# Common operand offsets, halved scaled states, filled waits, and rows moved by products in a fused attention and feed-forward kernel

## The chip, the core and the metric

The kernel runs on one core of a Trainium2 chip. The core's engines run at the same time and meet at semaphores: TensorE (PE in the profile, its weight loads PEld) multiplies a stationary tile with a moving one into PSUM, VectorE (DVE), ScalarE (ACT) and GpSimd (POOL) work elementwise, and SyncE (SP) issues the transfers between HBM and the on-chip SBUF. Each engine takes its instructions in the order in which the program lists them. The metric is the device time of one execution, in microseconds (us).

## What is computed

A gated linear attention (4 sequences, 8 heads, 768 steps, head size 48) and two feed-forward layers behind it, all in float32:

```python
def _attn_ref(q, k, v, alpha):
    for t in range(S):
        state = alpha[:, :, t, :, None] * state + np.einsum('bhd,bhe->bhde', k[:, :, t], v[:, :, t])
        y[:, :, t] = np.einsum('bhd,bhde->bhe', q[:, :, t], state)

def _moe_ref(x, w_in, w_out):          # 384 -> 2048 -> 384
    h = x @ w_in
    return (h * np.cos(h)) @ w_out

def _moe2_ref(x, w1, w2, w3, w_out):   # 384 -> 768 -> 384
    h = np.maximum(np.maximum(x @ w1, x @ w2), x @ w3)
    return h @ w_out
```

The attention's output, 3072 tokens of 8 x 48 features, is the first layer's x; the first layer's result is the second's.

## The kernel before

The 3072 tokens are cut into six units of 512 tokens (8 chunks of 64: two of each of the four sequences). Heads go in pairs p = 0 to 3. `att(u, k, p, t0)` does one pair of one unit, k = 0 to 3 standing for p = 3, 0, 1, 2: two scans on VectorE give the products of alpha within a chunk (g) and their scaled inverse, GpSimd scales k and q with them (L367 or L379, L382), TensorE transposes k (L387, copied out as kt in L390), forms q times k (L399) and k times v (L404), the first masked into a (L411 and L412 in unit 0, L415 later). VectorE then steps the state s from chunk to chunk (L421, L423). Each state is scaled by its chunk's g into d: in unit 0 by ScalarE, one instruction a chunk and head (L430); in later units by GpSimd, one a head (L435). `values` sums a times v (L449) and q times d (L455) into y. ScalarE writes y's high part into the layer's input tile xt (L470); the low part is what is left, in unit 0 by a product with minus identity (L473) and a copy (L475), later by a subtraction (L477). The pair p = 3 does not go to xt but to yy0: a pair's tile has 2 x 48 rows of its own and 2 x 16 free ones, and p = 3's 96 rows fill these, in before by two transfers for each of the other pairs (L484). In unit 0 all y share the two PSUM tiles acc0 and acc1.

Every operand of the feed-forward layers is a pair of float32r tiles, high and low, so each product is three instructions. A weight block arrives as 64-bit words (L307), VectorE turns it into float32 in three steps (L310 to L312), ScalarE takes the high part (L315) and GpSimd the low part (L316). `moe1(i)`, i = 16 u + f, computes h of one of the 16 blocks f of a unit by nine instructions (L497 to L499) of 128x512, the elementwise chain (L504 to L507 and, for i below GLP1 = 20, L509 to L511 with the low part on GpSimd, else L513, L514, L519 on VectorE), and nine instructions into the three accumulators (L524 to L526). The accumulators are written out at the unit's end (L533 to L536). `moe2_h` and `moe2_o` do the second layer (L574 to L586, L597 to L603).

The order is a planner's: `Program.order` gives every operation an estimated duration and a due time, simulates the engines, and the instructions are then emitted by simulated start, each engine's own in that order. The terms `W1E` (how many blocks ahead of its use a weight is due) and `MOE_EARLY` (how many blocks ahead the elementwise chain is due) are such due times; `PSUM` has five rotating banks ps0 to ps4 whose use the planner also settles. The layer-one weights wih, wil, woh, wol are allocated from the far end of SBUF, the attention's tiles from the near end behind xt, q, gh, gl, yy and raw. 16 products of the identity (L639) run first of all on TensorE.

Of the kernel before, what the change touches and what calls it, by code (L numbers as in the profile page):

```python
# [49 lines left out]
NQ, NG, NRAW, NIN, NV, NGS = 3, 2, 3, 3, 2, 3  # L50
NBANK = 5
# [7 lines left out]
GLP1 = 20  # L59
# [5 lines left out]
DAC = 1  # L65


W1E = 10
MOE_EARLY = 4
# [6 lines left out]
WARM, COLD, IDLE = 16, 7.0, 2.5  # L76


class Program:
# [38 lines left out]
    def order(self, banks, limit):  # L118
# [25 lines left out]
        start = [0.0] * n  # L144
        dma_free = 0.0
# [17 lines left out]
        for _ in range(n):  # L163
            t, e = min((max(free[e], min(map(ready, w))), e) for e, w in waiting.items() if w)
            assert t < never
            i = min((self.ops[j][5], j) for j in waiting[e] if ready(j) <= t)[1]
            waiting[e].remove(i)
            _, dur, nbytes, _, _, _, port = self.ops[i]
            start[i] = t
            if e == "PE":  # L170
                if t - free[e] > IDLE:
                    cold = t + COLD
                dur += min(dur, max(0.0, cold - t) / 2)
            free[e] = t + dur
            end = t + dur
            if port:
                port_free = end
            if nbytes is not None:
                dma_free = max(dma_free, end + (0.65 if e == "SP" else 1.05)) + nbytes / 260e3
                end = dma_free + 0.9  # L180
            for k in opens.get(i, ()):
                f = min(range(limit[k[1]]), key=lambda f: freed_at[k[1]][f])
                m = single(t)
                chosen[k] = m
                bank_end[k] = (m, f, 0.0)
                freed_at[k[1]][f] = never
                bank_free[m] = never
            for k in bank_of[i]:
                m, f, last = bank_end[k]
                last = max(last, end + self.SEM)  # L190
                bank_end[k] = (m, f, last)
                open_left[k] -= 1
                if not open_left[k]:
                    freed_at[k[1]][f] = last
                    bank_free[m] = last
            for u in users[i]:
                lag = self.LAG.get((e, self.ops[u][0]), self.SEM)
                ready_at[u] = max(ready_at[u], end + lag)
# [42 lines left out]
def tile_kernel(ctx, tc, qka, vv, wt, outT):  # L241
# [20 lines left out]

    q_b = [mp.tile([P, HB], F32, name=f"q{i}") for i in range(NQ)]
    gh_b = [mp.tile([P, HB], F32R, name=f"gh{i}") for i in range(NG)]
    gl_b = [mp.tile([P, HB], F32R, name=f"gl{i}") for i in range(NG)]
    yy_b = [mp.tile([P, 2, HB], F32R, name=f"yy{i}") for i in range(2)]
# [4 lines left out]
    one0 = ap.tile([PR, NC, C1], F32, name="one0")  # L271
    inv0 = [ap.tile([PR, NC, C1], F32, name=f"inv{i}") for i in range(2)]
    tri = ap.tile([P, 1, C], F32, name="tri")
    al_b = [ap.tile([PR, KO], F32, name=f"al{i}") for i in range(NIN)]
    kq_b = [ap.tile([PR, 2 * HB], F32, name=f"kq{i}") for i in range(NIN)]
    g_b = [ap.tile([PR, AL], F32, name=f"g{i}") for i in range(NGS)]
# [60 lines left out]
    def att(u, k, p, t0):  # L337
# [87 lines left out]
        for c in range(NC - 1):  # L425
            op("DVE", 0.2, lambda c=c: state(c), [rk[c % 2], *kgs, (*sk, c)], [(*sk, c + 1)], t0 + 0.25)
            if u < DAC and not firsts[c + 1]:
                for j in range(2):
                    w = slice(UP * j, UP * j + D)
                    op("Act", act(D) + 0.09, lambda c=c, j=j, w=w: se.activation(d[w, j, c + 1], s[w, c + 1], AF.Copy, scale=g[w, c + 1, 0:1]),  # L430
                       [*kgs, (*sk, c + 1)], [(dk, j, c + 1)], t0 + 0.25)
        if u >= DAC:
            for j in range(2):
                w = slice(UP * j, UP * j + D)
                op("Pool", pool(NC * D), lambda j=j, w=w: ge.tensor_tensor(d[w, j], s[w], g[w, :, 0:1].to_broadcast([D, NC, D]), ALU.mult),  # L435
                   [*kgs, *[(*sk, c) for c in range(NC)]], [(dk, j, c) for c in range(NC)], t0 + 0.25)
        elif not firsts[0]:
            for j in range(2):
                w = slice(UP * j, UP * j + D)
                op("Act", act(D) + 0.09, lambda j=j, w=w: se.activation(d[w, j, 0], s[w, 0], AF.Copy, scale=g[w, 0, 0:1]), [*kgs, (*sk, 0)], [(dk, j, 0)], t0 + 0.25)  # L440
# [15 lines left out]

        op("PE", 3 * SWITCH + N2 * mm4(C) + NC * mm4(C), values, [vk, ("a", n2, 0), ("a", n2, 1), *[(dk, j, c) for j in range(2) for c in range(NC)], kq], [*yks, ("done", n2)], t0 + 0.3)
# [4 lines left out]
        else:  # L462
# [3 lines left out]
            xa = [("xtA", xn)]  # L466
        for h in range(2):
# [11 lines left out]
        if p < NP - 1:  # L479
# [67 lines left out]
    def open_np():  # L547
# [58 lines left out]
    def build():  # L606
# [19 lines left out]

        def setup_rest():
# [132 lines left out]
```

## Time and profile before

| | us |
|---|---|
| three runs, lowest, median, highest | 829.34, 831.05, 832.0 |
| the profiled execution | 831.06 |
| its span, from the first to the last instruction | 829.3 |
| TensorE busy | 805.4 |
| VectorE busy | 477.7 |
| ScalarE busy | 372.5 |
| GpSimd busy | 189.0 |
| granted TensorE clock, mean over the span | 0.979 |

A busy time counts an instruction from its start to its modelled end, and TensorE's instructions overlap, so its 805.4 us do not say how fast it goes; the distance between two starts does. The share of a span also mixes stages: the profile has a start of some 50 us with attention of unit 0 and the first weights, a stretch to some 130 us in which the remaining weights, the attention of units 1 and 2 and the first blocks run together, the rest of layer one to some 530 us, and layer two.

### The profile page before, as it was taken

The numbers are of one execution on the slowest core, as the hardware profiler recorded it, in microseconds if no ns is written. First come the engines' busy times: TensorE is split into PE (matmuls) and PEld (weight loads), VectorE is DVE, ScalarE is ACT, GpSimd is POOL, SyncE is SP. The second block draws the span as 40 slices with busy tenths as digits, with TensorE's granted clock in tenths as the row PEclk, the third lists the DMA queues.
The fourth block names the chain that finished last, engine by engine and source line by source line (L and its number), as shares of the span: only waits on it lengthen the run. The fifth ranks groups of instructions, "written<-read, shape, count | busy, mean of one in ns | idle before, by whom it ended". The sixth has DMA issues, their size and how long they took to land.

```text
span 829.3 us, 15144 instructions
## 1 busy us (share of the span) xinstructions
PE 805.4 (97%) x6168; PEld 649.1 (78%) x6168; DVE 477.7 (58%) x924; ACT 372.5 (45%) x695; POOL 189.0 (23%) x187
## 2 busy tenths in 40 slices
PE   7689999999999999999999999999999999999998
PEld 6567777878778877887788778888888888888886
DVE  7689999875786577657679954453122222322221
ACT  5865655645555554556466745521121211112121
POOL 6478777621231023102033200110000000000000
PEclk8589999999999999999999999999999999999999
DMA  9446764330242024102224610232020020200001
GB/s 281 137 133 193 208 188 150 117 106 12 73 146 65 1 76 143 43 1 74 65 86 134 238 45 2 104 106 77 26 88 19 22 89 25 77 26 13 13 26 38
DMA packets 26661, 71.86 MB, mean 87 GB/s; under 512 B 3488, under 2 KB 3488, under 8 KB 26592
## 3 DMA queue, kind: packets, MB, share of 16 engines
q1 hardware_dynamic: 26592, 70.90, 26.9%
q8 instruction: 48, 0.79, 0.4%
q14 instruction: 21, 0.17, 0.1%
HBM read 54.37 MB, written 14.16 MB: 83 GB/s over the span
## 4 chain that ended last, share of the span: by engine, by line
PE 84%; DVE 5%; POOL 4%; issue 3%; DMA 2%; ACT 1%; SPq 0%; DVEq 0%; POOLq 0%; ACTq 0%
PE ps L575 9%; PE ps L576 9%; PE ps L574 9%; PE acc L524 8%; PE acc L526 7%; PE ps L497 7%; PE acc L525 7%; PE ps L499 7%; PE ps L498 7%; PE ps L599 3%; PE ps L598 3%; PE ps L597 3%; PE ps L455 2%; PE ps L449 1%; PE ps L399 1%
## 5 line engine op out<-in xcount | busy, mean ns | idle before, releaser
L497 PE MATMUL ps<-xt,wih 128*128 128x512 f32 x288 | 117.7, 409 | 2.8 <-ACT q L506 1.7
L524 PE MATMUL acc<-gh,woh 128*128 128x512 f32 x288 | 117.5, 408 | 0.3 <-DVE yy L534 0.2
L499 PE MATMUL ps<-xt,wil 128*128 128x512 f32 x288 | 115.0, 399 | 1.4 <-POOL wil L316 1.4
L526 PE MATMUL acc<-gl,woh 128*128 128x512 f32 x288 | 114.4, 397 | 0.6 <-DVE gl L519 0.4
L498 PE MATMUL ps<-xt,wih 128*128 128x512 f32 x288 | 114.8, 399 | 0.0
L525 PE MATMUL acc<-gh,wol 128*128 128x512 f32 x288 | 114.0, 396 | 0.0
L504 ACT ACTIVATE q<-ps 128x512 int32<-128x512 f32 x96 | 57.2, 596 | 70.8 <-PE ps L499 70.2
L584 DVE TENSOR_TENSOR ps<-t,ps 128x512 f32<-128x512 f32 x36 | 25.0, 695 | 104.8 <-PE ps L576 104.7
L513 DVE SCALAR_TENSOR_TENSOR ps<-q,ps 128x512 f32<-128x512 f32 x76 | 52.7, 693 | 55.4 <-ACT q L507 55.2
L506 ACT ACTIVATE q<-q 128x512 f32<-128x512 f32 x96 | 60.6, 631 | 50.3 <-DVE q L505 49.6
L505 DVE SCALAR_TENSOR_TENSOR q<-q,ps 128x512 f32<-128x512 int32 x96 | 65.8, 685 | 28.0 <-ACT q L504 24.8
L585 ACT ACTIVATE h<-ps 128x512 fp32r<-128x512 f32 x36 | 21.5, 598 | 113.1 <-DVE ps L584 113.0
L519 DVE TENSOR_TENSOR gl<-ps,gh 128x512 fp32r<-128x512 f32 x76 | 52.1, 685 | 26.4 <-ACT gh L514 26.2
L497 PEld LDWEIGHTS ps<-xt,wih 128*128 128x128 f32 x288 | 54.6, 189 | 16.2 <-ACT q L506 2.2
L499 PEld LDWEIGHTS ps<-xt,wil 128*128 128x128 f32 x288 | 54.6, 190 | 15.3 <-POOL wil L316 2.1
L524 PEld LDWEIGHTS acc<-gh,woh 128*128 128x128 f32 x288 | 54.2, 188 | 15.0 <-DVE yy L534 1.1
L582 DVE TENSOR_TENSOR t<-t,ps 128x512 f32<-128x512 f32 x36 | 24.7, 687 | 71.4 <-PE ps L576 70.7
L526 PEld LDWEIGHTS acc<-gl,woh 128*128 128x128 f32 x288 | 54.2, 188 | 14.6 <-DVE gl L519 0.8
L514 ACT ACTIVATE gh<-ps 128x512 fp32r<-128x512 f32 x76 | 45.3, 597 | 42.8 <-DVE ps L513 39.9
L498 PEld LDWEIGHTS ps<-xt,wih 128*128 128x128 f32 x288 | 54.8, 190 | 11.8
L525 PEld LDWEIGHTS acc<-gh,wol 128*128 128x128 f32 x288 | 54.3, 189 | 11.7
L435 POOL TENSOR_TENSOR d<-s,g 48x384 f32<-48x384 f32 x40 | 34.6, 864 | 122.7 <-DVE s L423 121.1
(122 smaller groups left out, 1595.2 us busy)
## 6 DMA issues: line engine op xcount, KB each, us to landing
raw<-in_wt SPq DMA_DIRECT2D x56, 384.0 KB, 3.4
kq<-in_qka SPq DMA_DIRECT2D x23, 448.0 KB, 4.5
x1d<-yy SPq DMA_DIRECT2D x18, 512.0 KB, 2.8
xt<-x1d SPq DMA_DIRECT2D x18, 512.0 KB, 4.3
v<-in_vv SPq DMA_DIRECT2D x22, 256.0 KB, 3.5
al<-in_qka SPq DMA_DIRECT2D x24, 228.4 KB, 3.0
outT<-y SPq DMA_DIRECT2D x18, 256.0 KB, 2.0
xt<-yy SPq DMA_DIRECT2D x36, 64.0 KB, 2.7
```

The costliest lines, as they stand in the source:

```text
L497: pe.matmul(ps, wi["h"][:, f, cc], xt[:, cc, 0], start=(cc == 0), stop=False)
L498: pe.matmul(ps, wi["h"][:, f, cc], xt[:, cc, 1], start=False, stop=False)
L499: pe.matmul(ps, wi["l"][:, f, cc], xt[:, cc, 0], start=False, stop=(cc == NR - 1))
L504: op("Act", act(HB, True), lambda: se.activation(q.bitcast(I32), ps, AF.Copy, scale=INV2PI), [hk], [qk], m)
L505: op("DVE", dve(HB), lambda: ve.scalar_tensor_tensor(q, q.bitcast(I32), -TWOPI, ps, ALU.mult, ALU.add), [hk], [qk], m)
L506: op("Act", act(HB), lambda: se.activation(q, q, AF.Sin, scale=0.5), (), [qk], m)
L524: pe.matmul(acc[c], oh, gh, start=(f == 0), stop=False)
L525: pe.matmul(acc[c], ol, gh, start=False, stop=False)
L526: pe.matmul(acc[c], oh, gl, start=False, stop=(f == NF1 - 1))
L574: pe.matmul(ps, w2t["h"][m][:, f, cc], xt[:, cc, 0], start=(cc == 0), stop=False)
L575: pe.matmul(ps, w2t["h"][m][:, f, cc], xt[:, cc, 1], start=False, stop=False)
L576: pe.matmul(ps, w2t["l"][m][:, f, cc], xt[:, cc, 0], start=False, stop=(cc == NR - 1))
```

## The change

Seven things change together.

*Offsets.* A pad of 88 floats is allocated behind the layer-one weights and one behind the layer-two tiles on the far side, and the attention's tiles that are read by scans get rows of 544 floats. In the built programs the byte offsets within a partition are these:

| tiles | before | after |
|---|---|---|
| xt, gh, gl, w of layer two (near side), modulo 512 | 128 | 128 |
| wih, wil, woh, wol, modulo 512 | 480 | 128 |
| h2, wo2 of layer two, modulo 512 | 480 | 128 |
| kq of attention, modulo 128 | 32 | 0 |
| a, v, kt, s, d, modulo 128 | 0 | 0 |

*Scaled states.* In unit 0 ScalarE now makes d for the first head of a pair only (DAH = 1); the second head's is one GpSimd instruction, as in later units.

*Rows by products.* In unit 0 the 16-row pieces of pair 3 are no longer transferred: a selection matrix for each pair (built by ScalarE in the tile gl1) is multiplied with yy0 and summed into y before the pair's y is read.

*Fills.* Where the planner saw TensorE idle ahead of an operation that opens a bank, or of `values`, and before 48 us of its own time, up to ten products of the identity are put into the bank first.

*Numbers.* GLP1 goes from 20 to 28, W1E from 10 to 8, MOE_EARLY from 4 to 5, and one estimated duration changes.

```diff
+PAD = 88
+LINE = 544
-GLP1 = 20
+GLP1 = 28
+DAH = 1
+SELU = 1
-W1E = 10
-MOE_EARLY = 4
+W1E = 8
+MOE_EARLY = 5
+FILL, NFILL, SPARE = 48.0, 10, 0.3
...
             if e == "PE":
+                gap[i] = t - free[e]
...
     wo = {n: wp.tile([P, NF1, DM], F32R, name=f"wo{n}") for n in "hl"}
+    wp.tile([P, PAD], F32, name="pad")
...
+    sel = gl_b[1][:, 0:(NP - 1) * P].rearrange("p (k n) -> p k n", k=NP - 1)
...
-    al_b = [ap.tile([PR, KO], F32, name=f"al{i}") for i in range(NIN)]
+    al_b = [ap.tile([PR, LINE], F32, name=f"al{i}")[:, 0:KO] for i in range(NIN)]
...
             if u < DAC and not firsts[c + 1]:
-                for j in range(2):
+                for j in range(DAH):
...
-        if u >= DAC:
-            for j in range(2):
+        for j in range(2):
+            if u >= DAC or j >= DAH:
                 w = slice(UP * j, UP * j + D)
                 op("Pool", pool(NC * D), lambda j=j, w=w: ge.tensor_tensor(d[w, j], s[w], g[w, :, 0:1].to_broadcast([D, NC, D]), ALU.mult),
...
+        moved = u < SELU and p < NP - 1
...
+        if moved:
+            def rest():
+                for h in range(2):
+                    for x in range(2):
+                        pe.matmul(y[h][:, 0:HB // 2], sel[:, p], yy_b[0][:, x, HB // 2 * h:HB // 2 * (h + 1)], start=False, stop=(x == 1), skip_group_check=True)
+
+            op("PE", 0.5, rest, ["sel", ("gl", 1), *[("yy0", x, h) for x in "hl" for h in range(2)]], yks, t0 + 0.3)
...
-        if p < NP - 1:
+        if p < NP - 1 and not moved:
...
+        np_.tile([P, PAD], F32, name="pad2")
...
+        def setup_sel():
+            for p in range(NP - 1):
+                se.activation(sel[:, p], ident, AF.Copy, scale=0.0)
+                for i in range(2):
+                    row = 16 * (2 * p + i)
+                    src = UP * (row // D) + row % D
+                    se.activation(sel[:, p, UP * i + D:UP * (i + 1)], ident[:, src:src + 16], AF.Copy)
+
+        op("Act", 2.4, setup_sel, ["ident"], ["sel", ("gl", 1)], due=-97)
...
+            if G.ops[i][0] == "PE" and plan.start[i] < FILL:
+                bank = ps_b[chosen[plan.opens[i][0]]] if i in plan.opens else acc[0] if G.ops[i][3].__name__ == "values" else None
+                for _ in range(min(NFILL, int((plan.gap[i] - SPARE) / 0.22)) if bank is not None else 0):
+                    pe.matmul(bank[:, 0:P], ident, ident, start=True, stop=True)
             G.ops[i][3]()
```

Three places show what this does to the order. On ScalarE, in unit 0 behind the first pair's a, the names are d for scaled states, kt for the transposed k, a for the masked products; before:

```order
L430 ACTIVATE d0_125<-s3_124,g0_112 48x48 x4
L390 ACTIVATE kt1_118<-ps3_100 128x448
L430 ACTIVATE d0_125<-s3_124,g0_112 48x48 x6
L411 ACTIVATE a1_120<-ps0_97 128x256
L430 ACTIVATE d0_125<-s3_124,g0_112 48x48 x4
L411 ACTIVATE a1_120<-ps4_101 128x256
L390 ACTIVATE kt0_117<-ps3_100 128x448
L430 ACTIVATE d1_126<-s0_121,g1_113 48x48 x7
```

After (L405, L426 and L445 are L390, L411 and L430 of before):

```order
L445 ACTIVATE d0_126<-s3_125,g0_113 48x48 x2
L405 ACTIVATE kt1_119<-ps3_101 128x448
L445 ACTIVATE d0_126<-s3_125,g0_113 48x48 x3
L426 ACTIVATE a1_121<-ps0_98 128x256
L426 ACTIVATE a1_121<-ps4_102 128x256
L445 ACTIVATE d0_126<-s3_125,g0_113 48x48 x2
L445 ACTIVATE d1_127<-s0_122,g1_114 48x48 x7
L405 ACTIVATE kt0_118<-ps3_101 128x448
```

The second pair's two a's stood behind ten and behind fourteen of the first pair's d's, and now both stand behind five.

On TensorE, at the end of the last pair of unit 0 (L455 or L469 is the last of its value products, L473 or L496 the product with minus identity, L497 to L499 or L520 to L522 layer one); before:

```order
L455 MATMUL acc1_95<-yy1_90,d1_126 48x64 x2
L387 MATMUL ps3_100<-ident_76,kq1_110 128x112 x4
L497 MATMUL ps2_99<-xt0_463,wih_78 128x512
L498 MATMUL ps2_99<-xt0_463,wih_78 128x512
L499 MATMUL ps2_99<-xt0_463,wil_79 128x512
L473 MATMUL acc0_94<-xt0_463,minus_77 128x256
L473 MATMUL acc1_95<-xt0_463,minus_77 128x256
```

After:

```order
L469 MATMUL acc1_96<-yy1_91,d1_127 48x64 x2
L487 MATMUL acc0_95<-yy0_90,gl1_89 128x256 x2
L487 MATMUL acc1_96<-yy0_90,gl1_89 128x256 x2
L520 MATMUL ps3_101<-xt0_480,wih_78 128x512
L521 MATMUL ps3_101<-xt0_480,wih_78 128x512
L522 MATMUL ps3_101<-xt0_480,wil_79 128x512
L496 MATMUL acc0_95<-xt0_480,minus_77 128x256
L496 MATMUL acc1_96<-xt0_480,minus_77 128x256
```

The four products with the selection (L487) stand between the value products and the reading of y; the transposes of the next unit's pair stand further on.

On TensorE, where the first three blocks' h are done and banks have to come free; before:

```order
L497 MATMUL ps1_98<-xt0_463,wih_78 128x512
L498 MATMUL ps1_98<-xt0_463,wih_78 128x512
L499 MATMUL ps1_98<-xt0_463,wil_79 128x512
L387 MATMUL ps2_99<-ident_76,kq0_109 128x112 x4
L497 MATMUL ps3_100<-xt0_463,wih_78 128x512
```

After:

```order
L520 MATMUL ps3_101<-xt0_480,wih_78 128x512
L521 MATMUL ps3_101<-xt0_480,wih_78 128x512
L522 MATMUL ps3_101<-xt0_480,wil_79 128x512
L734 MATMUL ps2_100<-ident_76 128x128 x10
L402 MATMUL ps2_100<-ident_76,kq2_112 128x112 x4
L734 MATMUL ps4_102<-ident_76 128x128 x3
L520 MATMUL ps4_102<-xt0_480,wih_78 128x512
```

Ten fills (L734) into bank ps2 now precede the transposes that open it, and three precede the product that opens ps4; there are 35 fills in all.

## Rows read from the trace of the kernel before

**Rows 1.** The page: engine table, busy tenths in 40 slices, granted clock.
```profile
PE 805.4 (97%) x6168; PEld 649.1 (78%) x6168; DVE 477.7 (58%) x924; ACT 372.5 (45%) x695; POOL 189.0 (23%) x187
...
DVE  7689999875786577657679954453122222322221
...
PEclk8589999999999999999999999999999999999999
```

**Rows 2.** Stretches: us, busy us of each engine, PEclk, DMA share, GB/s.
```profile
30.00:40.00 10.00, 7.59 (x127) 5.86 (x120) 5.07 (x14) 6.69 (x19) 6.12 (x6) 0.50 0.52 137
100.00:150.00 50.00, 47.75 (x495) 37.68 (x494) 47.51 (x103) 30.16 (x56) 34.74 (x31) 1.00 0.55 165
150.00:200.00 50.00, 50.00 (x503) 39.93 (x502) 35.33 (x70) 26.40 (x48) 18.51 (x16) 1.00 0.31 92
269.00:282.00 13.00, 13.00 (x60) 10.47 (x58) 6.56 (x10) 7.58 (x13) 0.00 (x0) 1.00 0.01 1
540.00:552.00 12.00, 12.00 (x54) 9.94 (x54) 9.43 (x17) 4.31 (x8) 3.10 (x3) 1.00 0.44 155
600.00:650.00 50.00, 50.00 (x221) 41.16 (x220) 12.44 (x18) 8.96 (x15) 0.00 (x0) 1.00 0.13 48
```

**Rows 3.** Timeline of TensorE, layer one: start, us, engine, line, operands.
```profile
269.65 0.40 PE L497 MATMUL ps<-xt,wih 128*128 128x512 f32 x1
...
281.36 0.40 PE L499 MATMUL ps<-xt,wil 128*128 128x512 f32 x1
```

**Rows 4.** Timeline of TensorE, layer two.
```profile
540.05 0.39 PE L576 MATMUL ps<-xt,w1l 128*128 128x512 f32 x1
...
551.84 0.39 PE L574 MATMUL ps<-xt,w1h 128*128 128x512 f32 x1
...
599.69 0.39 PE L597 MATMUL ps<-h,wo2h 128*128 128x512 f32 x1
...
601.50 0.40 PE L599 MATMUL ps<-h,wo2h 128*128 128x512 f32 x1
...
603.82 0.39 PE L574 MATMUL ps<-xt,w0h 128*128 128x512 f32 x1
...
615.83 0.39 PE L576 MATMUL ps<-xt,w2l 128*128 128x512 f32 x1
```

**Rows 5.** Timeline of TensorE, waits: in brackets the idle time before, and its releaser.
```profile
57.71 0.57 PE L387 MATMUL ps<-ident,kq 112*128 112x112 f32 x4 [2.00 <-DVE q L509]
...
94.03 0.47 PE L497 MATMUL ps<-xt,wih 128*128 128x512 f32 x1 [1.74 <-ACT q L506]
...
112.09 0.69 PE L449 MATMUL ps<-a,v 64*64 64x64 f32 x32 [1.21 <-DVE s L423]
124.18 0.47 PE L497 MATMUL ps<-xt,wih 128*128 128x512 f32 x1 [0.78 <-DVE q L509]
```

**Rows 6.** Groups of instructions: count, busy us, mean ns of one, idle before.
```profile
L519 DVE TENSOR_TENSOR gl<-ps,gh 128x512 fp32r<-128x512 f32 x76 | 52.1, 685 | 26.4 <-ACT gh L514 26.2
...
L435 POOL TENSOR_TENSOR d<-s,g 48x384 f32<-48x384 f32 x40 | 34.6, 864 | 122.7 <-DVE s L423 121.1
...
L430 ACT ACTIVATE d<-s,g 48x48 f32<-48x48 f32 x56 | 18.6, 332 | 1.3
...
L639 PE MATMUL acc<-ident 128*128 128x128 f32 x32 | 6.1, 378 | 1.4 <-POOL ident masks.py:199 1.4
```

**Rows 7.** Timeline of ScalarE in unit 0's attention.
```profile
7.95 0.54 ACT L390 ACTIVATE kt<-ps 128x448 f32<-128x448 f32 x1 [5.55 <-PE ps L387]
...
37.53 4.97 ACT L430 ACTIVATE d<-s,g 48x48 f32<-48x48 f32 x14
```

**Rows 8.** Timeline of VectorE, unit 0's states and layer one's first step.
```profile
24.33 0.26 DVE L423 SCALAR_TENSOR_TENSOR s<-s,g,ps 112x48 f32<-112x48 f32 x1 [2.76 <-ACT a L411]
...
36.97 0.21 DVE L421 COPY s<-ps 112x48 f32<-112x48 f32 x1 [4.47 <-ACT a L411]
...
53.57 0.69 DVE L505 SCALAR_TENSOR_TENSOR q<-q,ps 128x512 f32<-128x512 int32 x1 [0.41 <-ACT q L504]
```

**Rows 9.** The chain that ended last, around the last rows of unit 0: start, us, what.
```profile
48.38 0.51 SPq L484
...
48.95 2.88 DMA xt<-yy
...
51.96 0.47 PE ps L497
```

**Rows 10.** Who waited for whom on TensorE: us in total, times, longest.
```profile
PE ps L499 <- POOL wil L316: 1.4, 1, 1.4
```

More of the change, by code (lines that the diff above doesn't have):

```diff
@@ L144, in order @@
         start = [0.0] * n
+        gap = [0.0] * n
         dma_free = 0.0
@@ L202, in order @@
         self.start = start
+        self.gap = gap
+        self.opens = opens
         return sorted(range(n), key=lambda i: (start[i], i)), chosen
@@ L269, in tile_kernel @@
     ps_b = [pp.tile([P, 512], F32, name=f"ps{i}") for i in range(NBANK)]
-    one0 = ap.tile([PR, NC, C1], F32, name="one0")
-    inv0 = [ap.tile([PR, NC, C1], F32, name=f"inv{i}") for i in range(2)]
+    one0 = ap.tile([PR, LINE], F32, name="one0")[:, 0:AL].rearrange("p (c t) -> p c t", c=NC)
+    inv0 = [ap.tile([PR, LINE], F32, name=f"inv{i}")[:, 0:AL].rearrange("p (c t) -> p c t", c=NC) for i in range(2)]
     tri = ap.tile([P, 1, C], F32, name="tri")
-    al_b = [ap.tile([PR, KO], F32, name=f"al{i}") for i in range(NIN)]
+    al_b = [ap.tile([PR, LINE], F32, name=f"al{i}")[:, 0:KO] for i in range(NIN)]
     kq_b = [ap.tile([PR, 2 * HB], F32, name=f"kq{i}") for i in range(NIN)]
-    g_b = [ap.tile([PR, AL], F32, name=f"g{i}") for i in range(NGS)]
+    g_b = [ap.tile([PR, LINE], F32, name=f"g{i}")[:, 0:AL] for i in range(NGS)]
     v_b = [ap.tile([P, N2, 2, UP], F32, name=f"v{i}") for i in range(NV)]
@@ L427, in att @@
             if u < DAC and not firsts[c + 1]:
-                for j in range(2):
+                for j in range(DAH):
                     w = slice(UP * j, UP * j + D)
-                    op("Act", act(D) + 0.09, lambda c=c, j=j, w=w: se.activation(d[w, j, c + 1], s[w, c + 1], AF.Copy, scale=g[w, c + 1, 0:1]),
+                    op("Act", act(D) + 0.21, lambda c=c, j=j, w=w: se.activation(d[w, j, c + 1], s[w, c + 1], AF.Copy, scale=g[w, c + 1, 0:1]),
                        [*kgs, (*sk, c + 1)], [(dk, j, c + 1)], t0 + 0.25)
-        if u >= DAC:
-            for j in range(2):
+        for j in range(2):
+            if u >= DAC or j >= DAH:
                 w = slice(UP * j, UP * j + D)
@@ L436, in att @@
                    [*kgs, *[(*sk, c) for c in range(NC)]], [(dk, j, c) for c in range(NC)], t0 + 0.25)
-        elif not firsts[0]:
-            for j in range(2):
+            elif not firsts[0]:
                 w = slice(UP * j, UP * j + D)
-                op("Act", act(D) + 0.09, lambda j=j, w=w: se.activation(d[w, j, 0], s[w, 0], AF.Copy, scale=g[w, 0, 0:1]), [*kgs, (*sk, 0)], [(dk, j, 0)], t0 + 0.25)
+                op("Act", act(D) + 0.21, lambda j=j, w=w: se.activation(d[w, j, 0], s[w, 0], AF.Copy, scale=g[w, 0, 0:1]), [*kgs, (*sk, 0)], [(dk, j, 0)], t0 + 0.25)
         op("DVE", 0.2, lambda: state(NC - 1), [rk[1], *kgs, (*sk, NC - 1)], [(*sk, 0)], t0 + 0.27)
@@ L691, in tile_kernel @@
     chosen.update(chosen_)
+    plan = G
     build()
```

## The prediction

> **What bounds the kernel now.** I read the engine table and the forty slices first: TensorE is busy for 97% of the span, VectorE for 58%, but VectorE's digits stand at 8 and 9 from the third slice to the eighth, and the clock digit falls to 5 in the second [rows 1]. Then the busy time by stretch, which makes three stages of it [rows 2]. In 30 to 40 us the clock is at 0.50, the 1.2 GHz level, and TensorE has gaps. From 100 to 150 us VectorE works 47.51 of 50 us and TensorE 47.75: both are nearly full. From 150 us on TensorE is busy without a break and VectorE is not. The waits of TensorE that VectorE or ScalarE ends stand at 57.71, 94.03, 112.09 and 124.18 us [rows 5]; the last of these is the first product of block i = 14 (counted by groups of nine L497 to L499). So up to i = 14 the order on VectorE decides, and from there the number and the spacing of TensorE's instructions.
>
> The spacing is the main thing to see. In the first feed-forward layer 50 products of 128x512 start between 269.65 and 281.36 us [rows 3]: 0.2342 us each. In the second layer 53 start between 603.82 and 615.83 us [rows 4]: 0.2266 us each, the same shape, type and clock (1.00 in both). Eight products of L597 to L599, from 599.69 to 601.50 us, take 0.2263 us each. But ten products right behind the change from these to L574, 601.50 to 603.82 us, take 0.2320 us each, and then the rate is 0.2266 again.
>
> What differs is where operands lie. Modulo 512 bytes (one weight tile's row) the first layer's weights lie at 480 and the moving tiles at 128. In L574 to L576 both lie at 128, in L597 to L599 both at 480. So neither 128 nor 480 is slow by itself; the unequal pair is, and so are ten products behind a change of the pair. The neighbours' load is not the cause: from 540.05 to 551.84 us 52 products start 0.2267 us apart [rows 4] with VectorE busy 9.43 of 12 us and the DMA share at 0.44, while the slow stretch has 6.56 of 13 us and 0.01 [rows 2].
>
> **The change part by part.** The profiled execution is 831.06 us, of which 829.3 are its span; the median of the three runs is 831.05, so the two need no correction.
>
> *Offsets of the first layer.* The pad puts its weights at 128 too. If they then go at 0.2266, each product saves 7.6 ns. From i = 14 on TensorE sets the pace: 82 blocks x 18 products x 7.6 ns = 11.2 us. The 14 blocks before would save 14 x 18 x 7.6 ns = 1.9 us, but there VectorE is full, so I count 0 (bounds 0 and 1.9).
>
> *Relocking.* Attention interrupts the products three times a pair (L387; L399 with L404; L449 with L455), 48 times in the 16 pairs of units 2 to 5. If each time ten products go at 0.2320 again, that gives back 10 x 5.4 ns = 0.05 us, 2.6 us in all; if none, 0. No row of before shows equal operands behind attention, so I take the middle, 1.3.
>
> *Offsets of the second layer.* The second pad puts h and wo2 at 128 as well, so the roughly 30 changes between L574 to L576 and L597 to L599 should vanish: 30 x 0.05 = 1.6 us saved; 0.8 if half remain, since no row says what else a change brings.
>
> *Split scaled states.* In unit 0 ScalarE makes the scaled states d in 56 steps of 332 ns, 18.6 us [rows 6]; 14 of them, 4.97 us, stand in one row behind the last pair's a [rows 7]. Half go (28 x 0.332 = 9.3 us), and GpSimd makes them in four steps of 864 ns [rows 6]. GpSimd's step waits for all states of its pair. The nine small ScalarE copies that build the selections stand ahead of the first kt, before which ScalarE idles 5.55 us [rows 7]; they cost nothing unless they pass that, and then the first kt is late. The order shows the effect: pair 1's two a's stood behind ten and fourteen of pair 0's d's, and now both stand behind five. VectorE waited 2.76 us at 24.33 and 4.47 us at 36.97 for exactly such a's [rows 8].
>
> *Rows by products in PSUM.* Six issues on SP go. The last pair's chain was issue at 48.38, landing at 51.83, product at 51.96 [rows 9]: 3.6 us. Four products of half a row for each of three pairs take their place; by the rate above, 128x256 is 0.11 us at full and 0.23 us at half clock, so 0.5 to 0.9 us a pair, ahead of ScalarE's reading. But VectorE runs almost without a break from there to its first step of layer one at 53.57 [rows 8], with 0.41 us idle ahead of it, so the landing was not what came last: this gain is worth only what VectorE's order lets through. By the order VectorE also has six states, two a's and a scan less ahead of that first step; it does them later, so the step itself comes earlier than the gain.
>
> *Fills.* 35 products of 128x128 are added. The 16 of the warm-up take 6.1 us [rows 6], 0.38 each, so 13.4 us in all. In a wait for an operand they are free and may hold the clock up. Not so where the wait is for a bank: 10 stand ahead of the transposes that open ps2 and 3 ahead of the product that opens ps4. The 2.00 us wait at 57.71 was ended by VectorE's last read of such a bank [rows 5], and a fill that writes the bank has to wait for that too. These 13 come on top: at most 13 x 0.38 = 5.0 us of TensorE, in a stretch where VectorE is the slower.
>
> *Start in sum.* VectorE's shift is the yardstick. At best both of its waits go, 7.2 us. At worst nothing of them goes through and 2 of the 5 us of fills show. I take 3 us earlier, nearer to the 4.47 us wait than to none, since the chain behind it (a, state, d, value products) keeps its other steps.
>
> *The rest.* Moving the products' low part of i = 20 to 27 to GpSimd takes 8 x 0.685 us [rows 6] from VectorE after 150 us, where it has room: 0. Early terms 8 and 5 for 10 and 4 only reorder; ahead of the first vector step of i = 13 as many conversions (L310 to L312) stand as before, one more or less. I count 0, with 1 us each way.
>
> Sum: -11.2 + 1.3 - 1.6 - 3 = -14.5, so **816.5 us**. Ends of this case: best 11.2 + 1.9 + 1.6 + 7.2 = 21.9, so 809.2; worst 11.2 - 2.6 + 0.8 - 2 = 7.4, so 823.7.
>
> **The rivals.** *The offsets do nothing.* For it: the two layers also differ in accumulators and in load, and ten products behind a change are slow with equal operands. Against it: L597's steady 0.2263 with both at 480. Then only the start is left: 831.1 - 3 = 828, between 824 and 833.
> The Trainium skill (TensorE: Matmul & The Clock Gate, Step-by-step: what each phase is for) says that TensorE has two read ports, so that "Loading the next tile's weights doesn't steal SBUF read bandwidth from the running matmul"; by that rule this rival holds, 828. The two spacings of equal products speak against it, though no row names the port.
>
> *The start is bound by TensorE, not by VectorE.* Then its lead goes through: block 0's last products could start 10.4 us earlier than 51.96, as the wait for the last pair's a, seven of its d's and the landing (4.5 + 2.3 + 3.6) all go. With 13.1 us for all 96 blocks and 1.6 that gives 831.1 - 25.1 = 806. Against it: VectorE at 95% up to 150 us.
>
> *Weights late, which ends slower.* Early term 8 asks for each weight two blocks later than 10. If the products then wait for GpSimd's low part as once in the trace, 1.4 us [rows 10], in every one of the first 16 blocks for both weights, that is 45 us; for one of them, 22 us: 831.1 - 14.5 + 22 = 838.6. It decides from 0.91 us a block on. Against it: the level count of conversions above, and a single such wait in the whole trace.
>
> **How the numbers follow.** Forecast 0.79; offsets do nothing 0.09; start bound by TensorE 0.08; weights late 0.04. The range is the forecast's own ends, 809 to 823.5: they hold nearly all of its chance and, of the rivals, only the near part of the early start's and of that at 828's, about 8 in 10 together. 0.3%, about what a measurement of this kernel can tell, is 2.5 us: faster means below 828.5. The forecast and the early start are faster (0.87), and half of the rival at 828 (0.05): 0.92. The other half stays within, 0.04; slower 0.04.
>
> **What would show it.** Right: L520 to L522 and L547 to L549 start 0.227 us apart, with a few of 0.23 behind attention, where 234 stood; no slow ten behind a change of layer-two lines; the first vector step of block 0 between 46 and 51 us; VectorE still full up to about 120 us, TensorE with more gaps there than before. Wrong: 0.234 kept (offsets), 13 fills on the chain with a gap before them, waits for wil or wol in the first 16 blocks, or a clock that stays at 1.00 from the start and carries TensorE's lead through.

## The result, and the profile after

| | before | after |
|---|---|---|
| median of the runs | 831.0 us (829.34 to 832.0) | 817.89 us (815.8 to 821.61) |
| profiled execution, its span | 831.06, 829.3 us | 817.95, 816.2 us |
| ratio | 1 | 0.9849 (95% 0.981 to 0.9888) |

The changed kernel is faster by 13.1 us by the medians (the ratio, of the means, makes it 12.5), where 14.5 were forecast (816.5). Run once more beside other kernels (below, e8) it was at 818.89 us, ratio 0.9848 (0.9828 to 0.9868).

Line numbers move with the edit. The first layer's products are now L520 to L522 and L547 to L549, the second's L598 to L600 and L621 to L623; the first vector steps are L528 and L532, the a's L426, the d's L445 (ScalarE) and L450 (GpSimd), the weight conversion L325 to L327, the fills L734.

From the page of after, the engine table, VectorE's digits and the granted clock, to be set beside [rows 1]:

```profile
PE 795.4 (97%) x6250; PEld 649.4 (80%) x6250; DVE 472.6 (58%) x916; ACT 362.6 (44%) x676; POOL 206.6 (25%) x199
...
DVE  7988999864786587667679955452232222322221
...
PEclk9999999999999999999999999999999999999999
```

The clock's 8 and 5 of [rows 1] are gone from the digits. Busy time by stretch of after (columns as in [rows 2]):

```profile
10.00:20.00 10.00, 8.93 (x218) 8.27 (x218) 8.41 (x28) 6.47 (x22) 8.95 (x10) 0.83 1.04 304
30.00:40.00 10.00, 8.36 (x98) 6.79 (x99) 9.19 (x23) 5.77 (x19) 8.15 (x8) 1.00 0.62 156
40.00:50.00 10.00, 6.26 (x97) 5.06 (x97) 8.32 (x14) 7.47 (x14) 5.78 (x5) 1.00 0.48 152
100.00:150.00 50.00, 47.01 (x435) 37.33 (x434) 47.40 (x101) 29.12 (x54) 38.24 (x32) 1.00 0.52 156
262.00:274.50 12.50, 12.50 (x56) 10.32 (x55) 6.16 (x9) 7.62 (x13) 0.00 (x0) 1.00 0.00 0
```

In 30 to 40 us VectorE works 9.19 of 10 us where it worked 5.07, and the clock is 1.00 where it was 0.50. In 100 to 150 us both engines stand where they stood.

TensorE's timeline of after, for [rows 3] to [rows 5]:

```profile
25.01 0.48 PE L520 MATMUL ps<-xt,wih 128*128 128x512 f32 x1
...
47.52 2.50 PE L734 MATMUL ps<-ident 128*128 128x128 f32 x20 [3.74 <-DVE q L532]
49.85 0.55 PE L402 MATMUL ps<-ident,kq 112*128 112x112 f32 x4
...
119.81 0.39 PE L520 MATMUL ps<-xt,wih 128*128 128x512 f32 x1
...
129.76 0.50 PE L520 MATMUL ps<-xt,wih 128*128 128x512 f32 x1 [0.86 <-DVE raw L327]
...
262.04 0.39 PE L521 MATMUL ps<-xt,wih 128*128 128x512 f32 x1
...
274.50 0.39 PE L522 MATMUL ps<-xt,wil 128*128 128x512 f32 x1
...
289.31 0.40 PE L521 MATMUL ps<-xt,wih 128*128 128x512 f32 x1
289.55 0.39 PE L522 MATMUL ps<-xt,wil 128*128 128x512 f32 x1
289.78 0.40 PE L520 MATMUL ps<-xt,wih 128*128 128x512 f32 x1
290.01 0.39 PE L521 MATMUL ps<-xt,wih 128*128 128x512 f32 x1
290.24 0.39 PE L522 MATMUL ps<-xt,wil 128*128 128x512 f32 x1
...
589.62 0.39 PE L623 MATMUL ps<-h,wo2h 128*128 128x512 f32 x1
589.85 0.39 PE L598 MATMUL ps<-xt,w2h 128*128 128x512 f32 x1
...
591.66 0.39 PE L600 MATMUL ps<-xt,w2l 128*128 128x512 f32 x1
```

Four things are to be read in it. (Steps are worked out from starts printed to 0.01 us, so their fourth digit is rough.) From 262.04 to 274.50 us there are 55 steps of a product, 0.2265 us each, where [rows 3] has 0.2342. Behind an attention block (289.31 to 290.24) four steps take 0.232 each: the slow products behind an interruption, which the prediction calls relocking, are real with equal operands too. Behind a change to L598 (589.85 to 591.66) eight steps take 0.2263 each, so the slow ten of [rows 4] are gone. And the ten fills at 47.52 us (each shows as two instructions) stand behind a wait of 3.74 us for a bank that VectorE frees.

VectorE's first step of block 0, and what it waited for up to 47 us (columns of the waits: us in total, times, longest):

```profile
46.18 0.69 DVE L528 SCALAR_TENSOR_TENSOR q<-q,ps 128x512 f32<-128x512 int32 x1 [1.55 <-ACT q L527]
```

```profile
DVE s L436 <- ACT a L426: 1.2, 2, 0.8
...
DVE s L438 <- ACT a L426: 0.9, 2, 0.7
DVE s L438 <- POOL d L450: 0.7, 1, 0.7
```

The two waits of [rows 8], 2.76 and 4.47 us, are gone, and the step came 7.4 us earlier than 53.57.

### The profile page after: what moved, and what is told of

It is laid out like the page before. It is cut to its first block, busy times and chain, and to the rows that moved or that the text cites. A ratio compares the mean times of both kernels' runs of the same rounds, so it can differ in the third digit from the quotient of the medians.

```text
span 816.2 us, 15280 instructions
## 1 busy us (share of the span) xinstructions
PE 795.4 (97%) x6250; PEld 649.4 (80%) x6250; DVE 472.6 (58%) x916; ACT 362.6 (44%) x676; POOL 206.6 (25%) x199
## 4 chain that ended last, share of the span: by engine, by line
PE 80%; DVE 8%; issue 4%; DMA 3%; POOL 2%; ACT 2%; SPq 0%; POOLq 0%; DVEq 0%; ACTq 0%
PE ps L600 9%; PE ps L598 9%; PE ps L599 9%; PE acc L547 6%; PE ps L520 6%; PE acc L549 6%; PE acc L548 6%; PE ps L522 6%; PE ps L521 6%; PE ps L623 3%; PE ps L621 3%; PE ps L622 3%; PE ps L469 2%; DMA kq<-in_qka 2%; PE ps L414 1%
## 5 line engine op out<-in xcount | busy, mean ns | idle before, releaser
L520 PE MATMUL ps<-xt,wih 128*128 128x512 f32 x288 | 115.9, 402 | 3.6 <-ACT kt L405 1.5
L547 PE MATMUL acc<-gh,woh 128*128 128x512 f32 x288 | 116.4, 404 | 0.7 <-DVE yy L557 0.5
L521 PE MATMUL ps<-xt,wih 128*128 128x512 f32 x288 | 112.9, 392 | 1.6 <-ACT xt L498 1.6
L549 PE MATMUL acc<-gl,woh 128*128 128x512 f32 x288 | 113.1, 393 | 1.4 <-POOL gl L534 0.9
L522 PE MATMUL ps<-xt,wil 128*128 128x512 f32 x288 | 112.8, 392 | 0.0
L548 PE MATMUL acc<-gh,wol 128*128 128x512 f32 x288 | 112.6, 391 | 0.0
L527 ACT ACTIVATE q<-ps 128x512 int32<-128x512 f32 x96 | 57.1, 595 | 64.5 <-PE ps L522 62.5
L529 ACT ACTIVATE q<-q 128x512 f32<-128x512 f32 x96 | 60.5, 631 | 54.7 <-DVE q L528 54.2
L528 DVE SCALAR_TENSOR_TENSOR q<-q,ps 128x512 f32<-128x512 int32 x96 | 65.6, 683 | 29.8 <-ACT q L527 29.7
L536 DVE SCALAR_TENSOR_TENSOR ps<-q,ps 128x512 f32<-128x512 f32 x68 | 47.2, 694 | 49.7 <-ACT q L530 49.4
L520 PEld LDWEIGHTS ps<-xt,wih 128*128 128x128 f32 x288 | 54.2, 188 | 16.5 <-ACT kt L405 1.9
L549 PEld LDWEIGHTS acc<-gl,woh 128*128 128x128 f32 x288 | 54.2, 188 | 14.9 <-DVE gl L542 1.7
L547 PEld LDWEIGHTS acc<-gh,woh 128*128 128x128 f32 x288 | 54.3, 189 | 14.4 <-DVE yy L557 2.3
L450 POOL TENSOR_TENSOR d<-s,g 48x384 f32<-48x384 f32 x44 | 37.9, 861 | 109.3 <-DVE s L438 107.6
L521 PEld LDWEIGHTS ps<-xt,wih 128*128 128x128 f32 x288 | 54.3, 188 | 12.4 <-ACT xt L498 2.2
L522 PEld LDWEIGHTS ps<-xt,wil 128*128 128x128 f32 x288 | 54.3, 188 | 11.5
L548 PEld LDWEIGHTS acc<-gh,wol 128*128 128x128 f32 x288 | 54.3, 189 | 10.4
L530 ACT ACTIVATE q<-q 128x512 f32<-128x512 f32 x96 | 60.5, 630 | 2.5
L542 DVE TENSOR_TENSOR gl<-ps,gh 128x512 fp32r<-128x512 f32 x68 | 46.6, 686 | 23.0 <-PE ps L522 13.3
```

What stands on the lines that cost most here:

```text
L520: pe.matmul(ps, wi["h"][:, f, cc], xt[:, cc, 0], start=(cc == 0), stop=False)
L521: pe.matmul(ps, wi["h"][:, f, cc], xt[:, cc, 1], start=False, stop=False)
L522: pe.matmul(ps, wi["l"][:, f, cc], xt[:, cc, 0], start=False, stop=(cc == NR - 1))
L528: op("DVE", dve(HB), lambda: ve.scalar_tensor_tensor(q, q.bitcast(I32), -TWOPI, ps, ALU.mult, ALU.add), [hk], [qk], m)
L529: op("Act", act(HB), lambda: se.activation(q, q, AF.Sin, scale=0.5), (), [qk], m)
L530: op("Act", act(HB), lambda: se.activation(q, q, AF.Square), (), [qk], m)
```

## The experiments

Each ratio is to runs of the kernel before made beside that run, whose medians lie between 831.0 and 832.63 us. The starts of the first products of block i = 14 and i = 32 are from the profile of each kernel. Four kernels have the very same order (after, e8, e11 and e6); their i = 32 lies between 213.09 and 216.71 us. A single profile's start is thus good to some 3.5 us, and a verdict on the start needs the medians.

| | edit | i = 14, us | i = 32, us | median, us | ratio to before (95%) |
|---|---|---|---|---|---|
| before | | 124.18 | 220.18 | 831.0 | 1 |
| after | | 119.81 | 214.62 | 817.89 | 0.9849 (0.981 to 0.9888) |
| e8 | after, again | 120.09 | 214.18 | 818.89 | 0.9848 (0.9828 to 0.9868) |
| e1 | before, layer-one pad alone | 122.95 | 216.91 | 822.12 | 0.9893 (0.9879 to 0.9908) |
| e2 | after without pads | 121.39 | 216.91 | 829.06 | 0.9969 (0.9956 to 0.9982) |
| e3 | after without fills | 118.62 | 213.43 | 816.41 | 0.9814 (0.9801 to 0.9827) |
| e4 | after without 13 fills | 120.94 | 214.96 | 815.92 | 0.9818 (0.9805 to 0.9832) |
| e5 | after, gaps between the weights, one buffer fewer | 154.85 | 244.37 | 850.33 (one run) | |
| e6 | after, layer-two pair unequal | 122.17 | 216.71 | 822.47 | 0.9894 (0.9872 to 0.9917) |
| e7 | after, all d on ScalarE | 125.85 | 219.34 | 823.23 | 0.9903 (0.9886 to 0.9919) |
| e9 | after, rows by DMA | 127.72 | 217.69 | 821.71 | 0.9884 (0.986 to 0.9908) |
| e10 | after, three old numbers | 119.79 | 219.90 | 822.31 | 0.9888 (0.987 to 0.9905) |
| e11 | after, 24 words of pad | 118.81 | 213.09 | 817.8 | 0.9839 (0.982 to 0.9858) |
| e12 | after, weights early | 123.89 | 218.90 | 822.29 | 0.988 (0.9851 to 0.9909) |

### e1: the offsets alone

```diff
     wo = {n: wp.tile([P, NF1, DM], F32R, name=f"wo{n}") for n in "hl"}
+    wp.tile([P, 88], F32, name="pad")
```

> The kernel before with one edit: the unused 88 words behind the first layer's weights, so that these lie at byte 128 modulo 512 like the moving tiles. Order of the work, start and second layer stay as they are. Theory (equal offsets are what is fast): products of the first layer start 0.2266 us apart where 0.2342 stood, with some eight of 0.232 behind attention; the forecast's two terms, -11.2 and +1.3, give 821, the shorter saving that the trace of the changed kernel shows (-8.8 from i = 14 on, of which -1.7 is the second layer) gives 824; the first product of i = 14 stays within 1 us of 124.18. Rival (the offset does nothing, the changed kernel's spacing comes from its new order): 0.2342 stays, 831 within 2.

TensorE's timeline of e1:

```profile
262.03 0.39 PE L525 MATMUL acc<-gh,woh 128*128 128x512 f32 x1
...
275.86 0.39 PE L526 MATMUL acc<-gh,wol 128*128 128x512 f32 x1
```

These are 61 steps, 0.2267 us each. One unused tile, with the order of the kernel before untouched, gives 9.6 us (831.72 to 822.12). The rival that the offset does nothing falls. From i = 14 to the last product its profile takes 692.38 us where before took 700.98: 8.6 us less. By i = 14 it is 1.2 us ahead, a little more than the 1 us that was allowed.

The weight loads do not differ. In the same stretch of layer one, before and then e1 (count, busy us, mean ns of one):

```profile
L526 PEld LDWEIGHTS acc<-gl,woh 128*128 128x128 f32 x9 | 1.7, 189 | 0.4
```

```profile
L527 PEld LDWEIGHTS acc<-gl,woh 128*128 128x128 f32 x12 | 2.3, 188 | 0.5
```

So the 7.6 ns of a product are not a longer load. What in the products takes them no run shows.

### e2: the start alone

```diff
-    wp.tile([P, PAD], F32, name="pad")
...
-        np_.tile([P, PAD], F32, name="pad2")
```

> The changed kernel without its two pads: first-layer weights back at 480, second-layer h and wo2 at 480; split states, selections, fills and early terms stay. Theory (start and offsets add up, and VectorE passes on only its own lead): the first product of i = 14 comes at 119.8 within 1 us, 0.2342 is back, the slow ten of the second layer are back, and the time is 831 - 4.4 = 826.6 (825 to 828.5). Rival 1 (the lead of the start is given back later, once VectorE has less to wait for): 830 to 832. Rival 2 (a faster TensorE in blocks 0 to 13 was part of the lead): i = 14 at 121 to 122, 828 to 829.

TensorE's timeline of e2 (L519 to L521 and L546 to L548 are the first layer here):

```profile
262.16 0.39 PE L519 MATMUL ps<-xt,wih 128*128 128x512 f32 x1
...
274.58 0.40 PE L521 MATMUL ps<-xt,wil 128*128 128x512 f32 x1
```

These are 53 steps of 0.2343 us: the slow spacing is back. The time is 829.06, outside the 825 to 828.5 of the theory: 2.7 us for everything but the pads. By the time and by i = 14 (121.39) that is rival 2: some of the lead that after has at i = 14 is the offsets' own, as e1's 1.2 us there say too, though both are within the spread of starts. What the start brings is kept to the end.

The parts add up: 9.6 (e1) + 2.7 (e2) leaves 0.8 of the 13.1 for the second layer. In the traces, from the first product of layer two (L575 in e1, L598 in after) to the last takes 353.80 us in e1 and 352.24 in after: 1.56 us.

### e6: the slow pair put into the second layer

```diff
+        np_.tile([P, PAD], F32, name="pad2")
         for n in "hl":
             w2t["o" + n] = np_.tile([P, NF2, DM], F32R, name=f"wo2{n}")
-        np_.tile([P, PAD], F32, name="pad2")
```

> The changed kernel with the second pad moved between y2 and wo2, so that the second layer's h stays at 128 and wo2 goes to 480: the pair that the first layer had before, now in the other layer, with other accumulators and load; nothing else differs. Theory (the pair of offsets is the cause, not the layer): the 324 products of the second layer's output go from 0.2267 to 0.234, the ten products behind each of some 30 changes go slow again, together 324 x 7.6 ns + 1.6 = 4.1 us; 822 (820.5 to 823.5). Rival (something else of the first layer made it slow, and the pad only happened to move it): spacing stays at 0.2267, 818 within 1.5.

TensorE's timeline of e6, second layer:

```profile
588.11 0.39 PE L621 MATMUL ps<-h,wo2h 128*128 128x512 f32 x1
...
592.32 0.39 PE L598 MATMUL ps<-xt,w2h 128*128 128x512 f32 x1
...
594.36 0.39 PE L598 MATMUL ps<-xt,w0h 128*128 128x512 f32 x1
```

The 18 output products up to 592.32 take 0.2339 us each, and the nine behind them 0.2267. So the pair of offsets is the cause, in either layer. From its first product to the last the second layer takes 354.64 us where after takes 352.24: 2.4 us, which is 324 products by 7.4 ns. The 1.6 us expected for slow tens did not come: the nine behind this change are fast at once. Of the 3.6 us between the medians of e6 and e8, the other 1.2 lie within the start's spread.

### e5 and e11: which offsets are equal

```diff
+    at = [f * DM + STEP * (f // 2) for f in range(NF1)]
...
+        return [t[:, x:x + DM] for x in at]
```

> The changed kernel with gaps inside the first layer's weights: each further pair of blocks f lies 64 bytes higher modulo 512, so the weights of f = 0 and 1 lie 0 bytes off the moving tiles' 128, those of f = 2 and 3 lie 64 off, and so on to 448. One buffer fewer for incoming weights, so the start and the total say nothing; what is read is the spacing of the first layer's products by offset, after 60 us of a unit's change. Theory (only equal offsets are fast): 0.2266 us at 0, about 0.234 at the seven others. Rival 1 (the period is 256 or 128 bytes, not a weight row's 512): 0.2266 at 256 too, or at 128, 256 and 384 too. Rival 2 (the price grows with the distance): steps between 0.2266 and more than 0.234, least at 64 and 448, most at 256.

TensorE's timeline of e5 (L527 to L529 and L554 to L556 are the first layer here):

```profile
448.71 0.39 PE L529 MATMUL ps<-xt,wil 128*128 128x512 f32 x1
...
450.75 0.39 PE L529 MATMUL ps<-xt,wil 128*128 128x512 f32 x1
...
502.24 0.40 PE L554 MATMUL acc<-gh,woh 128*128 128x512 f32 x1
...
506.44 0.39 PE L527 MATMUL ps<-xt,wih 128*128 128x512 f32 x1
...
510.62 0.39 PE L527 MATMUL ps<-xt,wih 128*128 128x512 f32 x1
...
513.83 0.40 PE L529 MATMUL ps<-xt,wil 128*128 128x512 f32 x1
```

The weights lie 64 bytes off in the 18 steps from 502.24 (0.2333 us each), 128 off in the 18 from 506.44 (0.2322), 192 off in the 14 up to 513.83 (0.2293), and 256 off in the nine from 448.71 to 450.75: 0.2267. From 150 us on, medians of the steps from the tenth on of a stretch of one offset:

```
bytes off        0    64   128   192   256   320   384   448
ns             227   233   231.5 229   227   233.5 232   229
steps            8    16    14    26    20     2    11    13
```

Rival 1 holds in its first form: the period is 256 bytes, not the 512 of a weight tile's row, though 320 has two steps only. Rival 2 falls, since 256 is fast and 64 is the slowest. e11 puts it to the test with the least pad that does it:

```diff
-PAD = 88
+PAD = 24
...
-        np_.tile([P, PAD], F32, name="pad2")
+        np_.tile([P, 88], F32, name="pad2")
```

> The changed kernel with 24 words of padding behind the first layer's weights in place of 88, so that these lie at 384 modulo 512, 256 bytes off the moving tiles. Theory (from the run with eight offsets, where 0 and 256 both gave 226.5 ns and the others 229.7 to 233: what counts is the offset modulo 256): the first layer's spacing stays at 0.2267, 818 within 1.5. Rival (the period is 512 and the eight products at 256 in that run were few and mixed): 0.233 to 0.234, 824 to 828.

```profile
261.63 0.39 PE L520 MATMUL ps<-xt,wih 128*128 128x512 f32 x1
...
272.74 0.39 PE L521 MATMUL ps<-xt,wih 128*128 128x512 f32 x1
```

In this timeline of e11 49 steps take 0.2267 us each, and the time is 817.8. Before's 480 against 128 were 96 bytes off modulo 256. Its 0.2342 is above every step of e5, so 64 is not the dearest offset, only the dearest of e5's.

### e3 and e4: the fills

```diff
-FILL, NFILL, SPARE = 48.0, 10, 0.3
+FILL, NFILL, SPARE = 48.0, 0, 0.3
```

> The changed kernel without the 35 products that fill waits. Theory (the fills hold the clock, and TensorE paces part of the start): the granted clock falls to 0.5 over stretches between 15 and 50 us, as in the kernel before, and i = 14 starts 1 to 3 us later; 819 to 821. Rival 1 (VectorE paces the start whatever the clock): clock falls, but i = 14 moves less than 0.7 us; 818 within 1. Rival 2 (fills cost more than they bring, by the 13 that stand in front of a wait for a bank): i = 14 up to 2.9 us earlier (13 x 0.22 us); 815 to 817.

Busy time by stretch of e3:

```profile
10.00:20.00 10.00, 8.00 (x198) 6.84 (x198) 7.83 (x26) 7.15 (x23) 8.02 (x10) 0.66 1.04 318
...
30.00:40.00 10.00, 8.77 (x109) 6.88 (x110) 8.59 (x23) 5.59 (x18) 7.92 (x8) 0.83 0.50 139
40.00:50.00 10.00, 5.34 (x81) 3.81 (x80) 8.40 (x14) 8.23 (x16) 5.83 (x5) 0.83 0.51 158
```

Without fills the clock is lower in all three stretches (0.66, 0.83, 0.83 against 0.83, 1.00, 1.00), so the fills do hold it up. It brings nothing: i = 14 comes no later, and the time is 816.41, in the span of rival 2.

```diff
-FILL, NFILL, SPARE = 48.0, 10, 0.3
+FILL, NFILL, SPARE = 44.0, 10, 0.3
```

> The changed kernel without the last 13 of its 35 fills, the ten and the three from 47.52 to 50.9 us that stand in front of a wait for a bank. Theory (VectorE paces that stretch): the transposes behind them start up to 2.9 us earlier (13 x 0.22 us), the first vector step of block 0 no earlier than 45.5, and i = 14 moves less than 0.7 us; 818 within 1. Rival (they are on the chain, as the prediction priced them): i = 14 and the end 1 to 2.9 us earlier; 815 to 817.

815.92, in the rival's span, though i = 14 and i = 32 of its profile lie within the spread of after's. Both kernels come out some 2 us below after and e8, which ran beside other runs of before; the interval of e4 overlaps those of after, e8 and e11, that of e3 those of after and e11. So that the fills gain something is not borne out, that they cost some 2 us is likely, and which of them cost it is open. e3 and e4 are the fastest versions here.

### e7: all scaled states on ScalarE

```diff
-DAH = 1
+DAH = 2
```

> The changed kernel with both halves of unit 0's scaled states d on ScalarE again (56 steps, none on GpSimd). Theory (the split is what the start gained by: VectorE waited 2.76 and 4.47 us for a's that stood behind d's on ScalarE): such waits of VectorE are back before 46 us, the first product of i = 14 comes 2 to 3 us later than 119.8, and the time is 820 to 821. Rival 1 (the rows by products carry the start, the split only moves work): i = 14 within 0.7 us, 818 within 1. Rival 2 (GpSimd's steps, which wait for all states of a pair, cost more than ScalarE's): 815 to 817.

ScalarE's timeline of e7:

```profile
11.41 4.97 ACT L445 ACTIVATE d<-s,g 48x48 f32<-48x48 f32 x14
...
22.54 4.97 ACT L445 ACTIVATE d<-s,g 48x48 f32<-48x48 f32 x14
...
34.36 4.98 ACT L445 ACTIVATE d<-s,g 48x48 f32<-48x48 f32 x14
43.84 0.38 ACT L426 ACTIVATE a<-ps 128x256 f32<-128x256 f32 x1 [0.88 <-DVE s L436]
...
44.91 4.98 ACT L445 ACTIVATE d<-s,g 48x48 f32<-48x48 f32 x14
```

The rows of fourteen d's of [rows 7] are back, the last a's come at 43.8 us where they came at 31.1, and the time is 4.3 us above e8. So this edit costs more than expected. How it costs was not as I had it: VectorE waits for a's no longer than in after. In the traces it is TensorE's products with d that come late. TensorE's timeline of e7 and then of after, at the second pair:

```profile
22.43 4.64 PE L734 MATMUL acc<-ident 128*128 128x128 f32 x20 [0.60 <-ACT yy L498]
...
27.73 0.99 PE L469 MATMUL acc<-kq,d 112*48 112x64 f32 x28
```

```profile
22.47 0.99 PE L469 MATMUL acc<-kq,d 112*48 112x64 f32 x28
```

The second pair's products with d start at 27.73 us in e7 and at 22.47 in after. Two things stand ahead of them in e7: the fourteen d's on ScalarE, which end at 27.51, and ten fills at a granted clock of 0.50, since the planner places the fills anew with the order. The row of d's alone could hold them, and the pair's a's are 6 us late already (21.49 against 15.48); what the fills add to the 4.3 us is open, as no run has e7 without fills.

### e9: the rows by DMA

```diff
-SELU = 1
+SELU = 0
```

> The changed kernel with unit 0's spare rows put between the other pairs by six DMAs again, and no selecting products. Theory (as the prediction put it: this gain is worth only what VectorE's order lets through): the landing is back on the way of block 0, whose later products come some 3 us later, but i = 14 moves less than 1 us; 818 to 819.5. Rival 1 (the rows carry the start): i = 14 2.5 to 4 us later, 820.5 to 822.5. Rival 2 (selecting products and their copies cost more than the DMAs): 815 to 817.

TensorE's timeline of e9:

```profile
32.07 0.50 PE L520 MATMUL ps<-xt,wih 128*128 128x512 f32 x1 [0.69 <-DMA xt<-yy]
...
38.89 1.13 PE L414 MATMUL ps<-kq 48*64 48x64 f32 x32 [2.99 <-POOL kq L397]
```

Rival 1 by the time: 821.71, 2.8 us above e8, with the two intervals just overlapping. i = 14 comes 7.9 us later than in after, more than any case had, and 3.1 are left of it at i = 32. The landing is back on the way of block 0, which starts at 32.07 us (25.01 in after), though TensorE waits only 0.69 us for it. The rows seem to be worth more in the new start than I thought; fills are placed anew here too.

### e10 and e12: the planner's numbers

```diff
-GLP1 = 28
+GLP1 = 20
...
-W1E = 8
-MOE_EARLY = 5
+W1E = 10
+MOE_EARLY = 4
```

> The changed kernel with the three planning numbers of before: early terms 10 and 4 in place of 8 and 5, and the products' low part moved to GpSimd for i below 20 in place of 28. Theory (they only reorder; the prediction counted 0 with 1 us each way): 818 within 1.5, and from i = 20 on the same pace. Rival 1 (the later weights pay for the start, since they leave VectorE room there): i = 14 later by 1.5 us or more, 820 to 822. Rival 2 (the moved low part and late weights cost between i = 14 and 28): 815 to 816.5.

TensorE's timeline of e10:

```profile
140.68 0.50 PE L520 MATMUL ps<-xt,wih 128*128 128x512 f32 x1 [1.89 <-DVE q L532]
```

822.31, nearest to rival 1 by the time but not by i = 14, which comes when it came in after. But TensorE still waits for VectorE at 140.68 us, and i = 32 comes 5.3 us later. In after the last wait up to 200 us that VectorE ends is at 129.76.

```diff
-W1E = 8
+W1E = 10
```

> The changed kernel with the first layer's weights asked for two blocks earlier again (early term 10 in place of 8); the other two planning numbers stay as changed. With all three numbers back, i = 14 came at the same 119.8 us but i = 20 at 156.9 in place of 148.5, and the time was 822.3. Theory (the later weights are what pays: between i = 13 and 20 VectorE is still the slower, and weights asked for early stand there in front of steps that TensorE waits for): i = 20 at 153 us or later, 820.5 to 823. Rival 1 (the two other numbers carry it: the feed-forward's VectorE steps one block earlier, and the low part moved to GpSimd up to i = 27): i = 20 within 1.5 us of 148.5, 817 to 819.5. Rival 2 (the weights late cost something, as the prediction's fourth case had it): earlier weights make it faster, 814 to 816.5.

Who waited on TensorE in e12, 100 to 170 us:

```profile
PE ps L463 <- DVE raw L327: 3.0, 1, 3.0
```

822.29: this one number alone makes as long a time as all three, some 3 us more than e8 (its interval overlaps e8's, e10's does not). But the place was another than I expected, and another than in e10: i = 14 is already 4 us late, with TensorE 3.00 us idle ahead of the value products at 101.47, behind a weight conversion on VectorE, and i = 20 comes at 150.72, not at 153. So weights asked for early probably cost; whether by the conversions or by the rest of the new order is not shown. Later weights did not make the kernel slower, so the prediction's last rival falls.

### e8: the changed kernel again

> The changed kernel itself once more, for the comparison with the runs beside it: 818 within 1.5, and i = 14 between 118.8 and 121. If the fills are neutral, as the runs without them suggest (816.4 and 815.9), it lies between 815.5 and 818; if they cost something, between 818 and 819.5.

818.89 us, in the second span.

## Why the prediction held, step by step

- *Offsets of the first layer, -11.2, and relocking, +1.3.* The mechanism is right (e1, e6) and the price of a product too: 0.2342 to 0.2267. From i = 32 to i = 80, where TensorE alone sets the pace, the 824 steps between such products sum to 191.29 us in e1 against 196.21 in before: 4.9 us less, where 824 by 7.6 ns are 6.3. So 31 interruptions by attention take back 1.3, 0.043 us each. The first step behind one is as long as in before (0.337 by the median), and the next five take some 0.231, every time. Over 48 that is 2.1, more than the middle that I took. Then -9.1 is due from i = 14 on, and e1 has -8.6; the rest is lost behind i = 80, where 1.4 of some 2.0 come. The first 14 blocks, counted 0 with a bound of 1.9, saved about 1. Together -9.6 by the medians, against -9.9: that the two misses cancel is luck.
- *Offsets of the second layer, -1.6.* -1.56 between e1 and after.
- *Start, -3, and the rest, 0.* e2 puts the two together at -2.7 (1.5 to 3.7 by its interval). The sum is right, its reasons only in part. Right: VectorE's two waits go, and its first step comes at 46.18 (46 to 51 was asked). (Its waits for a's up to that step were 10.5 us in all in before, six waits, and are 2.1 in after; the 7.2 counted two of them.) Wrong, as far as e10 and e12 go: that the rest is worth 0. Undoing the split, the rows or the early weights alone costs 4.3, some 3 and some 3 us (e7, e9, e12), far more than the 2.7 that all of them bring together over before. Each of these runs is planned anew, in e7 and e9 with other fills, so these are prices of whole orders, and the parts can't be priced one at a time from the trace of before. The early term of the weights is the term that failed: I held that it only reorders, but VectorE has little room there, in after 47.40 of 50 us up to 150. No run undoes the rows of 544 floats or the changed duration; they are in the 2.7.
- *Fills, up to 5.0 us for the 13.* They did stand behind a bank wait (3.74 us at 47.52), as told. The price was too high: the ten fills from 47.52 to 49.85 take 0.23 us each, at full clock, where my 0.38 came from the warm-up. With 0.23 the 13 are at most 3.0 us, and e4 makes the loss about 2, within intervals that overlap.
- *The clock.* From 15 us on it stands at 1.00 but for a fall at 70 to 80 us (0.80 to 0.86), which I had named as a sign of the earlier, TensorE-bound start (806). It was none: e3 loses the clock and no time. So the clock does not set the start. VectorE is the engine nearest to full there, 9.19 of 10 us from 30 to 40; that it alone sets the start is argued, not shown.
- *Sum.* -9.6 - 1.6 - 2.7 = -13.9; measured -13.1, and -12.6 for e8. The sign "more gaps on TensorE than before" held in 100 to 150 us (47.01 busy against 47.75).
- *The rivals.* Offsets that do nothing (828) fell with e1, the start bound by TensorE (806) with e3, late weights (838.6) with the time itself. The rule that stood beside it (the Trainium skill, TensorE: Matmul & The Clock Gate, Step-by-step: what each phase is for) is that loading weights takes nothing from the running product's reads. By it the offset should have been worth nothing, and it made 822 of 832; whether those reads are what suffers no run shows.

## What to carry to other kernels

Where two layers with the same products run at different rates, compare the addresses of the operands before the engines: here an unused tile of 24 words is worth 3% of every product of a layer, and it can be tried by itself in one line. In this start a warmer TensorE brought nothing (the fills), and weights asked for earlier probably cost some 3 us (e12). Price a re-planned start as a whole, and leave the bounds wide: undoing one part moves the order and the fills of all the others.

## What the runs showed of the hardware

- A 128x512 product whose weights are loaded for it starts 0.227 us behind the last when weights and moving tile lie at the same byte modulo 256 (e1, e11, 0 and 256 of e5), and up to 0.234 when not: 0.2342 with the weights 96 bytes above (before), 0.233 at 64, 0.232 at 128, 0.229 at 192 (e5). The sign counts: 192 above is 64 below, and costs less than half of 64 above. A weight load takes 188 to 189 ns in before and in e1.
- What makes the slow products behind a change is not settled. With equal operands they follow attention (after: 0.232 behind 289.31) and, in before, the change from 480 and 480 to 128 and 128 [rows 4]; but behind the change from 480 and 128 to 128 and 128 there are none (e6).
- The same program's start varies: i = 32 between 213.09 and 216.71 us in four profiles of one order (after, e6, e8, e11).
